# The x buffers at the top end of SBUF, a norm and sixteen weight copies on other engines, and the late weights' steps reordered

## Chip, cores and metric

The kernel runs on one core of one Trainium2 chip. The metric is the time of the whole program on the device in microseconds (us). Runs of the kernel before: median 1708.15 us of three (1706.96 to 1709.29).

## Reference

Block-diagonal attention (chunks of 64 tokens) makes x; two feed-forward stages follow, the first with relu squared, the second with a rational function as its activation.

```python
q_c = q.reshape(B, H, nc, chunk, D)                    # 8, 8, 9, 64, 64; k_c, v_c alike
scores = scale * np.matmul(q_c, k_c.transpose(0, 1, 2, 4, 3))
attn = np.exp(scores - np.max(scores, axis=-1, keepdims=True))
attn = attn / (np.sum(attn, axis=-1, keepdims=True) + 1e-09)
out = np.matmul(attn, v_c)                             # -> x: 4608 tokens x 512

h = x @ w_in1                                          # 512 -> 2048
x = np.maximum(h, 0.0) ** 2 @ w_out1                   # 2048 -> 512

h = x @ w_in2; h2 = h * h; h3 = h2 * h
P = a[0] + a[1] * h + a[2] * h2 + a[3] * h3
Q = 1.0 + np.abs(b[0]) * np.abs(h) + np.abs(b[1]) * h2
out = (P / (Q + 1e-6)) @ w_out2
```

## The kernel before

**Tiling.** The 4608 tokens are 9 blocks of 512 (4 attention tiles of 128 each), the 2048 inner columns are 16 slices f of 128. A step s is one block b and one f; both feed-forward stages have 9 x 16 = 144 steps. Every float32 operand of these products is split into a high part of the type fp32r and a low part (the difference), and each product is three matmuls: low x high, high x low, high x high (`mm3`, L179). So `mm_h` (L185), h = x @ w_in for one step, is 4 x 3 = 12 matmuls into one PSUM bank, with a w slice stationary and x moving (512 columns). `mm_out1` (L191) and `mm_out2` (L197) add a step's contribution to four accumulators (acc), 12 matmuls as well: in stage 1 a w slice is stationary and g moves, in stage 2 a slice of g is stationary and w moves. TensorE runs h of step s and then acc of step s - 2 (stage 1) or s - 3 (stage 2), as `LAG` says. There are 2 x 2 x 144 such groups of 12.

**Order.** Nothing is left to a scheduler. `at(t, fn, ...)` puts an event at a time counted in steps, and `issue(until)` runs all events below that time in order of (time, place in the list); this order is the order of every engine's queue. An event's time says nothing of when its inputs are there: an engine works its queue in order and waits at each instruction for what it needs. All loads and stores go through SyncE's (SP) one queue.

**Weights.** The inputs w_in and w_out are 32 weight tiles of 512 columns, named (f, half): half 0 is a piece of w_in, half 1 a slice of w_out. h of a step reads two half 0 tiles (for f = 14 and 15 these are (14, 0) and (15, 0)); acc of a step reads the half 1 tile of its f. A weight comes as 64-bit words. `w_load` (L126) fetches them into a staging tile st (two buffers, once the early ones are through), `w_words` (L138) is two ScalarE (ACT) passes, `w_join` (L146) one VectorE (DVE) pass that joins the halves into wc, `w_split` (L151) copies the high part on the engine given and subtracts on GpSimd (POOL) for the low part. The join frees the staging tile. Of the 32 tiles, 24 are early; 8 are late: their SBUF space is taken over from the staging tiles of the early ones. In the order in which the kernel before works on them they are (10,1), (11,1), (14,0), (15,0), (12,1), (13,1), (14,1), (15,1), at the times `t_late + 0.65 * jl` with t_late = 10.4, jl = 0 to 7; the load is 1.3 earlier, the join 0.4 and the split 0.8 later (L543 to L551). Even ones copy on ACT, odd ones on POOL.

**Attention.** It is spread over stage 1: per tile, two transposes or loads of q and k, scores (`mm_s`), max, exp, sum (`s_sum`, L339, whose last instruction makes z), `s_norm` (L345), a transpose of e, the product with v, and `x_evac` (L378), which writes a tile of x. For tiles 4 to 7 the norm is on POOL and e is transposed by TensorE (`f_tr`, L360), then copied by `f_copy` (L370), half on ACT and half on DVE; the tiles' q and k come by `tr_second` (L298). From tile 8 on the norm is on DVE. Their q and k come by `load_qk` (L266) in units of 192 tokens; unit 1 is 8 calls of 4 DMAs, so 32 pieces, at the event times 10.3 to 10.86.

**Passage to stage 2.** While stage 1's last block runs, `w_in2` and `w_out2`, joined earlier and kept in DRAM, are loaded into the same 32 tiles (`w2_load`); `w2_split` (L172) then copies the high part, half 0 on ACT and half 1 on DVE, and subtracts on POOL. Stage 2's activation is `e1` to `e4` (L390 to L431).

**SBUF.** From the bottom, a partition holds 384 bytes of scratch and constants, x (4 tiles of 8192), g (6 of 2048), r (2048), 24 early weights (4096 each, from 47,488 to 145,792), co (128 bytes), and from 145,920 the early staging tiles (32 KB), which the 8 late weights replace; in stage 2 t2 and ev lie where attention's pools at the right end were given up. The right end, where the pools with side="right" begin, is 229,344.

Of the kernel before, what the change touches and what calls it, by code (L numbers as in the profile page):

```python
# [26 lines left out]
def attn_moe_moe_kernel(  # L27
# [25 lines left out]
    nc = tc.nc  # L53
# [10 lines left out]
    NS = NBLK * NF  # L64
    scale = 1.0 / float(D) ** 0.5

    xs = ctx.enter_context(tc.tile_pool(name="xs", bufs=1))
    g_p = ctx.enter_context(tc.tile_pool(name="g", bufs=3))
    r_p = ctx.enter_context(tc.tile_pool(name="r", bufs=1))
    dram_p = ctx.enter_context(tc.tile_pool(name="scr", bufs=1, space=DRAM))  # L70
# [5 lines left out]

    w_order = sorted([(f // 2 * 2, f, 0) for f in range(NF)] + [(f + LAG[0] + 0.5, f, 1) for f in range(NF)])
    n_first, n_late = 2, 8
    late = [(half, f) for _, f, half in w_order[-n_late:]]
    W = {(half, f): const.tile([128, 2, DM], F32R, name=f"w{half}_{f}")  # L80
         for half in range(2) for f in range(NF) if (half, f) not in late}
# [8 lines left out]
    def at(t, fn, *args):  # L90
        events.append((t, len(events), fn, args))

    def issue(until):
        events.sort(key=lambda e: e[:2])
        with tc.manual_schedule():
            while events and events[0][0] < until:
                _, _, fn, args = events.pop(0)
                fn(*args)

    def tl(pool, shape, dt, nm, tag=None):  # L100
        return P[pool].tile(shape, dt, name=nm, tag=tag or nm)
# [396 lines left out]
    def attention(t, t0):  # L498
        if t < 2 * TPB:
            at(t0 - 1.45, tr_second, t)  # L500
            at(t0 - 1.2, tr_copy, t, "q", nc.vector)
            at(t0 - 1.2, tr_copy, t, "k", nc.vector)
        else:
            at(t0 - 1.0, tr, t, "qs", "q")
            at(t0 - 0.9, tr, t, "ks", "k")
        at(t0 - 1.5, load_tok, t, v, "v", f"v{t % 2}")
        at(t0, mm_s, t, t)
        at(t0 + 0.2, s_max, t)
        at(t0 + 0.45, s_exp, t)
        at(t0 + 0.6, s_sum, t)  # L510
        if t < 2 * TPB:
            at(t0 + 0.8, s_norm, t, nc.gpsimd)
            at(t0 + 1.5, f_tr, t, "aps")
            at(t0 + 1.6, f_copy, t)
        else:
            at(t0 + 0.9, s_norm, t, nc.vector)
            at(t0 + 1.1, s_tr, t)
# [6 lines left out]
    for t in range(TPB, NTILE + 1):  # L524
        b, i = divmod(t, TPB)
        slot[t] = slot1(i) if b == 1 else 14.9 + 3.14 * i if b == 2 else NF * (b - 1) - 4.55 + 4 * i
        at(slot[t], a_ps, t)
        if t > TPB:
            at(slot[t], mm_pv, t - 1, t)
            at(slot[t] + 0.3, x_evac, t - 1, nc.vector)  # L530
        if t < NTILE:
            attention(t, slot[t])

    for u in range(len(UNITS)):
        t0 = slot[(sum(UNITS[u - 2]) - 1) // 128] - 0.8 if u >= 2 else slot[2 * TPB - 2 + u] - 1.3
# [5 lines left out]
    t_late = -0.6 + 0.5 * (NF * 2 - n_late - n_first)  # L541

    for j in range(n_first, 2 * NF):  # L543
        key = w_keys[j]
        jl = j - (2 * NF - n_late)
        t = -0.6 + 0.5 * (j - n_first) if jl < 0 else t_late + 0.65 * jl
        if j >= 6:
            at(t - (1.3 if jl >= 0 else 2.6), w_load, *key)
        at(t, w_words, key)
        at(t + 0.4, w_join, key)  # L550
        at(t + 0.8, w_split, key, (nc.scalar, nc.gpsimd)[j % 2])  # L551

    for s in range(NS):
        at(s, mm_h, s)
# [12 lines left out]
    for f in range(NF):  # L567
        for half_, t in ((0, NS - NF + f // 2 * 2 + 1.6), (1, NS - NF + f + LAG[0] + 0.95)):
            at(t, w2_load, f, half_)
            at(t + 2.1 + (f * 0.3, f * 0.6)[half_], w2_split, f, half_, (nc.scalar, nc.vector)[half_])  # L570

    at(NS - 100, init2)
    for b in range(NBLK):
# [18 lines left out]
    def pool(stack, name, bufs, **kind):  # L592
        P[name] = stack.enter_context(tc.tile_pool(name=name, bufs=bufs, **kind))

    with ExitStack() as p1:
        pool(p1, "attn", 1, side="right")
        pool(p1, "w", 2, side="right")
        pool(p1, "wc", 2, side="right")
        pool(p1, "ev", 2, side="right")
        P["ident"] = tl("attn", [128, 128], F32, "ident")  # L600
        with ExitStack() as p0:
            pool(p0, "ws", 6)
            pool(p0, "wcs", 4)
            with ExitStack() as p00:
                pool(p00, "aps", 1, space=PSUM)
                issue(-10)
            pool(ctx, "acc", 1, space=PSUM)
            ACC += [P["acc"].tile([128, 512], F32, name=f"acc{i}", tag=f"acc{i}") for i in range(4)]
            pool(p1, "aps", 1, space=PSUM)
            issue(t_late + 0.35)  # L610
        pool(ctx, "wlate", 1)
        W.update({k_: P["wlate"].tile([128, 2, DM], F32R, name="w%d_%d" % k_, tag="w%d_%d" % k_) for k_ in late})
        issue(T_P2)
# [33 lines left out]
```

## Time and profile before

| what | value |
|---|---|
| median of three runs | 1708.15 us |
| profiled execution, time of the whole program | 1708.93 us |
| its span on the core | 1707.2 us |
| mean granted TensorE clock | 0.988 of full speed |
| TensorE (PE) busy | 1662.9 us, 97%, 9312 instructions |
| VectorE (DVE) busy | 1118.3 us, 66% |
| ScalarE (ACT) busy | 918.3 us, 54% |
| GpSimd (POOL) busy | 361.4 us, 21% |

How to read it: the profile is one execution, and its span is the time between the first and the last instruction on the core; the rest of the program's time lies around it. PE is TensorE's matmuls, PEld its weight loads, SPq the queue of SyncE, which issues the DMAs. L181 is line 181 of the kernel printed above. A row of the timeline gives the start, the duration and, in brackets, the idle time of that engine just before with what ended it. Stage 2 begins with step 144, and weights are exchanged between about 880 and 980 us.

### The profile page before, as it was taken

Reading aid. Unit: us, or ns where it says so; the run is one execution under the profiler, and the core shown is the slowest. Engines: PE = TensorE matmul, PEld = TensorE weight load, DVE = VectorE, ACT = ScalarE, POOL = GpSimd, SP = SyncE. Lnnn points to the kernel's source line nnn. Section 1 sums busy time; section 2 is a strip of 40 time slices with the busy share of each in tenths; the row PEclk is TensorE's granted clock in tenths of the full one; section 3 lists DMA queues with packets and bytes.
Section 4 is the critical chain, followed back from the end, with each engine's and each line's share of the span. In section 5 each row is a group of like instructions: output and inputs, shape, how many; then the busy total and the mean of one; then the engine's idle time right before and its main releaser. Section 6 shows DMA issues by size and latency. Waiting matters only on the chain.

```text
span 1707.2 us, 24454 instructions
## 1 busy us (share of the span) xinstructions
PE 1662.9 (97%) x9312; PEld 1352.2 (79%) x9312; DVE 1118.3 (66%) x1820; ACT 918.3 (54%) x1482; POOL 361.4 (21%) x290
## 2 busy tenths in 40 slices
PE   6898999999999999999999999999999999999998
PEld 4686888888788888888887788888888888888886
DVE  5765765556655566652118987777777777777776
ACT  5654333333333233322327677777777777777775
POOL 2542000000000000000565423232323232323222
PEclk8998999999999999999999999999999999999999
DMA  9544334334234343210431010101010101000000
GB/s 240 173 106 124 83 75 122 79 99 109 61 94 103 79 123 68 68 35 1 136 99 62 1 50 1 50 1 50 1 50 0 50 0 42 9 25 26 0 26 25
DMA packets 213190, 108.58 MB, mean 64 GB/s; under 512 B 182224, under 2 KB 182224, under 8 KB 211920
## 3 DMA queue, kind: packets, MB, share of 16 engines
q1 hardware_dynamic: 213072, 107.01, 23.3%
q8 instruction: 73, 1.20, 0.3%
q14 instruction: 45, 0.37, 0.1%
HBM read 79.69 MB, written 27.26 MB: 63 GB/s over the span
## 4 chain that ended last, share of the span: by engine, by line
PE 88%; DVE 6%; ACT 2%; DMA 1%; issue 1%; SPq 1%; POOL 0%; POOLq 0%; DVEq 0%; ACTq 0%
PE acc L181 15%; PE h L183 14%; PE h L181 14%; PE h L182 14%; PE acc L183 14%; PE acc L182 14%; PE a L323 1%; PE a L314 1%; DVE t L415 1%; DVE t L395 1%; SPq L272 1%; DVE w L416 1%; DVE wc L148 1%; DVE g L421 0%; DMA st<-in_moe_w_in_dram 0%
## 5 line engine op out<-in xcount | busy, mean ns | idle before, releaser
L181 PE MATMUL h<-x,w 128*128 128x512 f32 x1152 | 454.7, 395 | 13.4 <-DVE w L410 6.7
L182 PE MATMUL h<-x,w 128*128 128x512 f32 x1152 | 451.9, 392 | 0.4 <-DVE x L110 0.4
L183 PE MATMUL h<-x,w 128*128 128x512 f32 x1152 | 452.2, 393 | 0.0
L227 ACT ACTIVATE r<-h 128x512 f32<-128x512 f32 x144 | 86.0, 597 | 406.3 <-PE h L183 399.6
L110 POOL TENSOR_TENSOR gl<-g,gh 128x512 fp32r<-128x512 f32 x144 | 186.4, 1295 | 548.1 <-ACT gh L105 540.0
L107 DVE CAST gh<-r 128x512 fp32r<-128x512 f32 x144 | 67.5, 469 | 314.8 <-ACT r L228 309.2
L181 PEld LDWEIGHTS h<-x,w 128*128 128x128 f32 x1152 | 217.9, 189 | 63.4 <-DVE w L410 9.3
L182 PEld LDWEIGHTS h<-x,w 128*128 128x128 f32 x1152 | 218.2, 189 | 47.6 <-DVE x L110 0.9
L183 PEld LDWEIGHTS h<-x,w 128*128 128x128 f32 x1152 | 217.9, 189 | 47.2
L181 PE MATMUL acc<-gh,w 128*128 128x512 f32 x576 | 231.1, 401 | 3.2 <-POOL w L110 2.0
L181 PE MATMUL acc<-w,gl 128*128 128x512 f32 x576 | 226.7, 394 | 1.6 <-POOL gl L110 1.6
L395 DVE SCALAR_TENSOR_TENSOR t<-h,co,t 128x512 f32<-128x512 f32 x144 | 125.2, 870 | 155.8 <-ACT t L394 155.7
L183 PE MATMUL acc<-gh,w 128*128 128x512 f32 x576 | 227.0, 394 | 0.0
L182 PE MATMUL acc<-gl,w 128*128 128x512 f32 x576 | 227.0, 394 | 0.0
L183 PE MATMUL acc<-w,gh 128*128 128x512 f32 x576 | 225.5, 391 | 0.0
L182 PE MATMUL acc<-w,gh 128*128 128x512 f32 x576 | 225.3, 391 | 0.0
L110 POOL TENSOR_TENSOR gl<-r,gh 128x512 fp32r<-128x512 f32 x16 | 21.6, 1350 | 693.0 <-DVE gh L107 693.0
L105 ACT ACTIVATE gh<-g 128x512 fp32r<-128x512 f32 x144 | 91.2, 633 | 96.7 <-DVE g L421 96.7
L181 PEld LDWEIGHTS acc<-gh,w 128*128 128x128 f32 x576 | 109.0, 189 | 29.4 <-POOL w L110 2.7
L181 PEld LDWEIGHTS acc<-w,gl 128*128 128x128 f32 x576 | 108.1, 188 | 29.0 <-POOL gl L110 2.4
L183 PEld LDWEIGHTS acc<-gh,w 128*128 128x128 f32 x576 | 109.1, 189 | 24.3
L182 PEld LDWEIGHTS acc<-gl,w 128*128 128x128 f32 x576 | 109.4, 190 | 22.6
(76 smaller groups left out, 2279.7 us busy)
## 6 DMA issues: line engine op xcount, KB each, us to landing
st<-in_moe_w_in_dram SPq DMA_DIRECT2D x32, 512.0 KB, 4.1
st<-in_moe_w_out_dram SPq DMA_DIRECT2D x32, 512.0 KB, 4.3
x2d<-ev SPq DMA_DIRECT2D x36, 256.0 KB, 2.4
x<-x2d SPq DMA_DIRECT2D x9, 1024.0 KB, 4.8
out_dram<-ev SPq DMA_DIRECT2D x36, 256.0 KB, 2.2
v<-in_v_dram SPq DMA_DIRECT2D x32, 256.0 KB, 4.3
w2d<-wc SPq DMA_DIRECT2D x32, 256.0 KB, 2.8
w<-w2d SPq DMA_DIRECT2D x32, 256.0 KB, 2.6
```

Source lines behind the costliest of these rows:

```text
L105: nc.scalar.activation(out=o, in_=x, func=ACTF.Copy)
L107: eng.tensor_copy(out=o, in_=x)
L110: eng.tensor_tensor(out=o, in0=x, in1=hi.bitcast(F32), op=ALU.subtract)
L148: nc.vector.scalar_tensor_tensor(out=c, in0=c, scalar=3, in1=st[:, :, 0], op0=ALU.logical_shift_left, op1=ALU.bitwise_or)
L181: nc.tensor.matmul(out=o, lhsT=al, rhs=bh, start=first and i == 0, stop=False)
L182: nc.tensor.matmul(out=o, lhsT=ah, rhs=bl, start=False, stop=False)
L183: nc.tensor.matmul(out=o, lhsT=ah, rhs=bh, start=False, stop=last and i == len(pairs) - 1)
L227: nc.scalar.activation(out=r, in_=ps, func=ACTF.Relu)
L272: nc.sync.dma_start(out=T[nm, "unit", u][32 * Q:32 * Q + 32, hp, :n // 32], in_=src[bb, 2 * hp + Q // 2, ss:ss + n, 32 * (Q % 2):32 * (Q % ...
L314: nc.tensor.matmul(out=o[half(c), h, p], lhsT=q_[half(h), p, half(c)], rhs=k_[half(h), p, half(c)], start=True, stop=True)
L323: nc.tensor.matmul(out=o[half(h), c, p], lhsT=v_[half(c), 2 * p + h], rhs=a_[h][half(c), :, p], start=True, stop=True)
L395: nc.vector.scalar_tensor_tensor(out=t, in0=h2, scalar=co[:, 5:6], in1=t, op0=ALU.mult, op1=ALU.add)
```

## The change

Five things are changed, none of which alters what is computed.

- The pool of x, xs, is put at the right end of SBUF. Everything on the left lies 32,768 bytes lower for that, and x starts at 196,576.
- The norm of tiles 4 to 7 is issued on DVE instead of POOL.
- The eight late weights are the same tiles, in the order (10,1), (14,0), (15,0), (11,1), (12,1), (13,1), (14,1), (15,1). Their steps are 0.6 apart instead of 0.65, the join 0.25 and the split 0.5 behind the words, and all eight copies of the high part are on ACT.
- The cut between the first part of the order, in which the early staging tiles live, and the second lies at 10.70 instead of 10.75.
- The 16 copies of half 1 in `w2_split` are on ACT instead of DVE.

```diff
-    xs = ctx.enter_context(tc.tile_pool(name="xs", bufs=1))
+    xs = ctx.enter_context(tc.tile_pool(name="xs", bufs=1, side="right"))
...
     n_first, n_late = 2, 8
+    w_order[-n_late + 1:] = sorted(w_order[-n_late + 1:], key=lambda u: (u[2], u[0]))
...
         if t < 2 * TPB:
-            at(t0 + 0.8, s_norm, t, nc.gpsimd)
+            at(t0 + 0.8, s_norm, t, nc.vector)
...
-        t = -0.6 + 0.5 * (j - n_first) if jl < 0 else t_late + 0.65 * jl
+        t = -0.6 + 0.5 * (j - n_first) if jl < 0 else t_late + 0.6 * jl
         if j >= 6:
             at(t - (1.3 if jl >= 0 else 2.6), w_load, *key)
         at(t, w_words, key)
-        at(t + 0.4, w_join, key)
-        at(t + 0.8, w_split, key, (nc.scalar, nc.gpsimd)[j % 2])
+        at(t + (0.4 if jl < 0 else 0.25), w_join, key)
+        at(t + (0.8 if jl < 0 else 0.5), w_split, key, nc.scalar if jl >= 0 else (nc.scalar, nc.gpsimd)[j % 2])
...
             at(t, w2_load, f, half_)
-            at(t + 2.1 + (f * 0.3, f * 0.6)[half_], w2_split, f, half_, (nc.scalar, nc.vector)[half_])
+            at(t + 2.1 + (f * 0.3, f * 0.6)[half_], w2_split, f, half_, nc.scalar)
...
-            issue(t_late + 0.35)
+            issue(t_late + 0.3)
```

## Rows read from the trace of the kernel before

**Rows 1.** The page, parts 1, 2 and 4: busy us, share of the span and instructions of each engine; the clock granted to TensorE in 40 slices of the span, in tenths of full speed; the chain of work that ended last, its shares by engine.

```profile
PE 1662.9 (97%) x9312; PEld 1352.2 (79%) x9312; DVE 1118.3 (66%) x1820; ACT 918.3 (54%) x1482; POOL 361.4 (21%) x290
PEclk8998999999999999999999999999999999999999
PE 88%; DVE 6%; ACT 2%; DMA 1%; issue 1%; SPq 1%; POOL 0%; POOLq 0%; DVEq 0%; ACTq 0%
```

**Rows 2.** What PE waits for, from the view of waits: the first three rows from the span's first 170 us, the last from 880 to 990 us. Columns: what waits, for what; us in total, times, the longest in us.

```profile
PE a L367 <- POOL e L347: 6.4, 2, 4.0
PE h L181 <- POOL w L110: 5.9, 1, 5.9
PE acc L181 <- POOL w L110: 2.0, 1, 2.0
...
PE h L181 <- DVE w L410: 6.7, 5, 2.5
```

**Rows 3.** One stretch of the passage to stage 2 in the view of windows: the stretch and its length; busy us and instructions of PE, PEld, DVE, ACT and POOL; the granted clock; the busy share of the DMA engines; GB/s.

```profile
940.00:960.00 20.00, 17.62 (x71) 14.34 (x72) 19.09 (x24) 13.94 (x23) 9.50 (x7) 0.91 0.00 1
```

**Rows 4.** The start of each group of 12 matmuls in a stretch of stage 2, from PE's timeline, by the group's first matmul: acc of f=9, h of f=13 (of the same block), acc of f=10, h of f=14, acc of f=11, h of f=15. The last row is the view of windows over the block of 16 steps to which they belong, with the columns of rows 3.

```profile
1058.09 0.39 PE L181 MATMUL acc<-w,gl 128*128 128x512 f32 x1
...
1060.81 0.39 PE L181 MATMUL h<-x,w 128*128 128x512 f32 x1
...
1063.53 0.40 PE L181 MATMUL acc<-w,gl 128*128 128x512 f32 x1
...
1066.32 0.40 PE L181 MATMUL h<-x,w 128*128 128x512 f32 x1
...
1069.11 0.40 PE L181 MATMUL acc<-w,gl 128*128 128x512 f32 x1
...
1071.91 0.40 PE L181 MATMUL h<-x,w 128*128 128x512 f32 x1
...
1011.85:1099.72 87.87, 87.87 (x386) 71.92 (x384) 67.79 (x99) 65.84 (x103) 25.75 (x20) 1.00 0.06 25
```

**Rows 5.** The timeline around the norm of tile 5, all engines. The last row is one line's instructions under L347, the norms on DVE of the tiles from 8 on: lowest, median and highest ns, first and last start.

```profile
77.35 0.20 DVE L343 RECIPROCAL z<-z 128x8 f32<-128x8 f32 x1
77.47 2.10 DVE L148 SCALAR_TENSOR_TENSOR wc<-wc,st 128x512 int32<-128x512 int32 x2
77.72 1.30 POOL L347 TENSOR_TENSOR e<-e,z 128x512 f32<-128x512 f32 x1 [2.22 <-DVE z L343]
...
78.16 0.63 ACT L105 ACTIVATE w<-wc 128x512 fp32r<-128x512 f32 x1 [2.12 <-DVE wc L148]
...
79.08 1.12 PE L367 MATMUL a<-ident,e 128*128 128x128 f32 x4 [3.96 <-POOL e L347]
...
84.38 0.63 PE L290 MATMUL a<-ident,qn 128*128 128x128 f32 x4 [0.61 <-DVE ah L107]
...
L347 DVE TENSOR_TENSOR e<-e,z x28: 684/692/694, 154.1 to 763.2; 128x512 f32<-128x512 f32 x28
```

**Rows 6.** SyncE's queue in the timeline, around the loads of (14,0) (at 112.11) and (15,0) (at 125.71).

```profile
112.11 0.39 SPq L131 DMA_DIRECT2D st<-in_moe_w_in_dram  x1
...
116.91 8.70 SPq L272 DMA_DIRECT2D ks<-in_k_dram  x16
125.71 0.39 SPq L131 DMA_DIRECT2D st<-in_moe_w_in_dram  x1
```

**Rows 7.** The timeline around the late weights, all engines: the join of (10,1); the first matmul of acc of f=11 in block 0; the first words' pass of (15,0); the high and the low part of (14,0); the first matmul of h of f=14; the twelfth of the same group; the first of h of f=15.

```profile
108.75 1.80 DVE L148 SCALAR_TENSOR_TENSOR wc<-wc,st 128x512 int32<-128x512 int32 x1
...
125.49 0.48 PE L181 MATMUL acc<-gh,w 128*128 128x512 f32 x1
...
129.73 0.66 ACT L141 ACTIVATE wc<-st 128x512 f32<-128x512 f32 x1 [10.24 <-DMA st<-in_moe_w_in_dram]
...
131.98 0.61 ACT L105 ACTIVATE w<-wc 128x512 fp32r<-128x512 f32 x1
...
132.67 1.71 POOL L110 TENSOR_TENSOR w<-wc,w 128x512 fp32r<-128x512 f32 x1 [10.12 <-ACT w L105]
...
134.44 0.80 PE L181 MATMUL h<-x,w 128*128 128x512 f32 x1 [5.90 <-POOL w L110]
...
139.31 0.63 PE L183 MATMUL h<-x,w 128*128 128x512 f32 x1
...
147.56 0.51 PE L181 MATMUL h<-x,w 128*128 128x512 f32 x1
```

**Rows 8.** The weights' high parts made by DVE in the passage to stage 2, as one line of the view of the tile w (lowest, median and highest ns, first and last start), and the timeline around one of them, ACT, DVE and POOL.

```profile
L107 DVE CAST w<-w x10: 420/1026/1074, 886.9 to 977.3; 128x512 fp32r<-128x512 f32 x10
...
926.75 0.58 ACT L393 ACTIVATE h<-h 128x512 f32<-128x512 f32 x1
926.92 1.30 POOL L110 TENSOR_TENSOR gl<-g,gh 128x512 fp32r<-128x512 f32 x1 [3.36 <-ACT gh L105]
927.23 0.68 ACT L394 ACTIVATE t<-h,co 128x512 f32<-128x512 f32 x1
...
927.47 1.03 DVE L107 CAST w<-w 128x512 fp32r<-128x512 f32 x1
...
928.42 0.74 DVE L395 SCALAR_TENSOR_TENSOR t<-h,co,t 128x512 f32<-128x512 f32 x1
929.09 1.78 DVE L415 SCALAR_TENSOR_TENSOR t<-t,r 128x512 f32<-128x512 f32 x1
```

## The prediction

> **What bounds the kernel now.** The page comes first: TensorE (PE) is busy 97% of the span and the chain of work that ended last is 88% PE, with the granted clock at full speed in nearly every slice [rows 1]. So only two things move the time: moments in which PE waits or runs at half clock, and the pace of its 6912 matmuls of 512 columns. The waits of PE show where it stands still: 6.4 us for the norm on POOL (two waits), 5.9 and 2.0 us for late weights, 6.7 us for VectorE (DVE) where stage 2 begins [rows 2]. After the longer of these waits the clock is low for a while: 0.91 of full speed on the mean in a stretch of the transition [rows 3].
>
> Then the pace. Each group is 12 matmuls on one PSUM bank, and the timeline gives group lengths by subtraction of starts [rows 4]: acc of f=9 2.72 us, h of f=13 2.72, acc of f=10 2.79, h of f=14 2.79, acc of f=11 2.80. PE is busy for the whole of such a block, at a clock of 1.00, so nothing waits [rows 4]. The slow groups are those that read one of the eight late weights, all others (not broken by attention work or an eviction) take 2.72. In h the late weight is the stationary operand, in stage 2's acc the moving one; both are slow. What differs is where these tiles lie. Height alone is unlikely: the weight of f=9 ends 128 bytes below that of f=10, one at 2.72 and one at 2.79, so its limit would have to lie in those 128 bytes. What co's 128 bytes do change is the offset against the other operand: x, g and the 24 early weights all start at 384 modulo 512, the late ones at 0.
>
> **The change, part by part.** I sum against the profiled execution, 1708.93 us (span 1707.2 and 1.73 around it); the median of the three runs shown is 1708.15, 0.78 less, and the forecast goes by that.
>
> *x at the top.* No instruction is added. Everything on the left moves down by 32,768 bytes, so g, early and late weights keep their offsets against each other; so do t2, ev and the pools that they replace, and no wait arises there. x itself starts at 196,576, that is 480 modulo 512: 96 bytes off the early weights, in each of the 16 h groups of a block. The trace shows two offsets only: 0 (2.72) and 128 either way (2.79 to 2.80). 96 is nearer to 128 than to 0, so I take the slow pace for h: 14 groups of f=0 to 13 that are fast today, 18 blocks, 0.075 us each = **+18.9 us** (0.07 to 0.08: 17.6 to 20.2). h of f=14 and 15 is already slow, acc stays as it is. Bounds: 0 if x's offset doesn't matter; below nothing, -18.9 by symmetry, since no row shows that 2.72 is the floor.
>
> *Norm of tiles 4 to 7 on DVE.* Tile 5 is the dear one [rows 5]. DVE ends z at 77.55; POOL's norm runs 77.72 to 79.02 and PE starts at 79.08. A norm on DVE takes 0.69 against 1.30, so the transposes start 0.8 us earlier. But two weight joins stand behind it on DVE and move by 0.69. The ScalarE (ACT) copy at 78.16 waits for the first join; two word steps, two activations and ACT's half of the ah copies follow it in ACT's queue, DVE's half comes later still, and PE's transposes at 84.38 wait for it. So 0.8 won at 79 is lost at 84. DVE no longer waits behind POOL's norm (the second join), but its next ops meet POOL's weight splits elsewhere. Tile 4 goes likewise with 0.2 won; tiles 6 and 7 are not waited for. I take **+0.3 us** (-0.8 to +1.2).
>
> *Late weights.* The order of SyncE's (SP) queue decides [rows 6]. Today: the load of (14, half 0) after the first 8 of 32 q/k pieces, the other 24, then at 125.71 the load of (15, half 0), whose words start on ACT at 129.73; behind those words ACT holds the copy of weight 14 (131.98) and POOL its low part (132.67 to 134.38), for which PE waits until 134.44 [rows 7]. New order by times of events: (10,1), (14,0), 4 q pieces, (15,0), 28 pieces, (11,1). Weights 14 and 15 are in time, but (11,1) now stands behind 28 pieces of 8.70 / 16 = 0.544 us, 15.2 us. (15,0) ahead of them needs the staging buffer that (10,1)'s join frees, today at 108.75 + 1.80 = 110.55, then up to 1.2 us later as the relu split of step 10 comes first. So (11,1) is issued at 126.2 to 127.5, words 4.0 us later; by today's starts ACT needs 131.98 - 129.73 = 2.25 for the words and the relu and square of step 12, then 0.6 for the copy, and POOL 1.7 [rows 7]: PE goes on at 134.7 to 136.1. It now stands before acc of f=11, ready at 125.49, one group earlier than today's wait. From there to h of f=15: three groups (8.2), attention (1.1) and 1.6 to 3.2 for half clock (today 11 spacings of matmuls right after the wait take 139.31 - 134.44 = 4.87, 0.443 each, where 2.72 / 12 = 0.227 is usual [rows 7]), so 145.6 to 148.4 against 147.56 today, where the second wait of 2.03 falls away. Mid: **-0.7 us** (-3.0 with the join as early as today and a short half clock, +1.5). The closer steps behind it gain nothing: what they start from has not landed. All eight casts on ACT instead of four lie in its idle time. The tile's last q/k loads come out within 2 us of today's and are not waited for by PE. Moving the cut from 10.75 to 10.70 moves no early weight's step across it.
>
> *The 16 half-1 casts on ACT.* Ten show as a group on DVE from 886.9 to 977.3, up to 1.07 us each [rows 8]. Follow one: POOL's gl holds until 928.22, so the cast (927.47) ends at 928.50 and the next op starts at 928.42. On ACT the extra copy (about 0.5 from start to start, as 926.75 to 927.23) goes ahead of the next step's activations, so t is ready at 927.23 + 0.68 + 0.5 = 928.41: the same moment. The POOL subtraction of that weight, now not waiting for DVE, follows gl at once and holds up the next DVE op instead of the one after (929.09, 1.78 against 0.69). So the cast was cover for a wait, not its cause. I take **-0.3 us** for the five waits (6.7 us); ends -3.5 (half of them gone [rows 2]) and +1.0 (subtractions that become ready earlier fall on steps that are now free).
>
> Sum: +18.9 + 0.3 - 0.7 - 0.3 = +18.2, so 1727.1 for an execution such as the profiled one and **1726 us** against the median.
>
> **Rivals.** *(a) x's place costs nothing*: the pace hangs on something else about late tiles. Against it: the same instruction has two paces by tile, with no wait [rows 4]. The Trainium skill, SBUF — State Buffer, section "SBUF: two separate sides", says that contention arises only at the port pair shared by VectorE and GpSimd and that PE has ports of its own and never waits; by that rule the x move is worth nothing. The rows give 2.72 and 2.79, so it doesn't tell the whole, yet it may hold for 96 bytes. Time: 0.3 - 0.7 - 0.3 = -0.7, 1707.5 (ends -7.3 and +3.7, most of it 1703.5 to 1711). *(b) Faster*: late tiles are slow for their place, x is not touched, and 32 KB lower they run at 2.72: 8 groups x 18 x 0.075 = -10.8, so 1696.7. It decides if late groups fall to 2.72. Against it the 128 bytes above; for it, that nothing shows x's sensitivity. *(c) Height after all, for x too*: +18.9 for h, -6 x 18 x 0.075 = -8.1 for acc: 1718.3. *(d) The late weights' steps do not come closer at all*, since SP's queue sets them; it is in my term already, worth 1.5 us either way.
>
> **How the numbers follow.** Forecast (own range 1719 to 1731): 0.43. (a) 0.35, of which 0.05 falls under 1704.7 and 0.03 over 1711.6; (b) 0.15; (c) 0.07. A measurement of this kernel tells about 0.2%, 3.4 us, from no change. Faster: 0.15 + 0.05 = 0.20. Same: 0.35 - 0.08 = 0.27. Slower: 0.43 + 0.07 + 0.03 = 0.53. The range 1703 to 1731 takes in the forecast, (a) and (c), and leaves out (b) and the tails.
>
> **What would show it.** x: h groups of f=0 to 13 at 2.79 to 2.80 in the timeline, a block of 16 steps near 89 us instead of 87.87 [rows 4]; at 2.72 the forecast is wrong by some 19 us and (a) stands; acc of f=10 to 15 at 2.72 means (b) or (c). Norm: the PE transposes near 79.08 come 0.8 earlier, those near 84.38 do not. Late weights: one PE wait of 9 to 10 us before acc of f=11, none before h of f=14. Casts: PE waits for L410 of 6 to 7 us in total again; if they fall under 4 us, DVE's own time was the cause and I was wrong there.

## The result and the profile after

The changed kernel takes 1731.06 us (median of 4 runs, 1730.01 to 1731.92) against 1707.56 for the kernel before (4 runs): 1.0132 times as long, 95% interval 1.0119 to 1.0145, +23.5 us. The forecast was 1726 with an own range of 1719 to 1731, inside a wider one of 1703 to 1731; the median stands 0.06 us above the upper end of both. The sign and the mechanism were right, but the main term, x at the top, was too small: +18.9 was forecast and the move of x alone measures +23.4.

In the changed kernel every line number is one higher than before (L182 is the first matmul of `mm3`). The page, the lines that answer to [rows 1]:

```profile
PE 1687.6 (98%) x9312; PEld 1354.6 (78%) x9312; DVE 1102.1 (64%) x1808; ACT 929.3 (54%) x1502; POOL 349.4 (20%) x282
...
PEclk8998999999999999999999999999999999999999
...
PE 91%; DVE 4%; ACT 2%; DMA 1%; issue 1%; SPq 1%; POOL 0%; POOLq 0%; DVEq 0%; ACTq 0%
```

PE is 24.7 us longer busy with the same 9312 matmuls at the same clock, and PE has a larger share of the chain that ended last. So the time is lost inside the matmuls, not between them. The span grew from 1707.2 to 1729.1. What PE waits for, whole run, answering to [rows 2]:

```profile
PE acc L182 <- POOL w L111: 8.8, 1, 8.8
PE a L368 <- DVE e L348: 5.1, 2, 3.0
PE h L182 <- DVE w L411: 5.0, 3, 2.6
```

Those waits have become shorter: 18.9 us in all, where the four rows of before come to 21.0. In the passage to stage 2 the clock is what it was [rows 3]:

```profile
940.00:960.00 20.00, 17.40 (x69) 13.71 (x68) 15.80 (x19) 14.57 (x24) 11.41 (x9) 0.91 0.00 0
```

The pace is what changed. PE's timeline in stage 2, the first matmul of the same groups as in [rows 4], that is acc of f=9, h of f=13, acc of f=10, h of f=14, acc of f=11, h of f=15, and after them the view of windows over one block of 16 steps, from its first h to that of the next block:

```profile
1069.28 0.40 PE L182 MATMUL acc<-w,gl 128*128 128x512 f32 x1
...
1072.04 0.40 PE L182 MATMUL h<-x,w 128*128 128x512 f32 x1
...
1074.86 0.39 PE L182 MATMUL acc<-w,gl 128*128 128x512 f32 x1
...
1077.66 0.40 PE L182 MATMUL h<-x,w 128*128 128x512 f32 x1
...
1080.45 0.40 PE L182 MATMUL acc<-w,gl 128*128 128x512 f32 x1
...
1083.25 0.40 PE L182 MATMUL h<-x,w 128*128 128x512 f32 x1
...
1088.85:1178.26 89.41, 89.41 (x386) 71.98 (x385) 67.33 (x99) 65.88 (x103) 25.70 (x20) 1.00 0.07 25
```

By subtraction, h of f=13 takes 2.82 us where it took 2.72; h of f=14, already slow, takes 2.79 as before. And acc of f=9 takes 2.76 where it took 2.72, although neither of its operands has moved against the other. The block takes 89.41 instead of 87.87, with PE busy throughout at a clock of 1.00.

From the starts of the first h of each block, before and after, the 21.9 us of the span lie as follows: +1.2 ahead of block 0, -0.5 in block 0, +8.4 in blocks 1 to 7, +1.5 in block 8, -0.9 in block 9 (the passage), +10.7 in blocks 10 to 16, +1.5 in the last. The first 1.2 are not the change's: that first h comes at 33.2 and at 34.2 in two of the kernels below that differ only in padding (shift_all and co_pad). Nor can block 0 be read to better than about 2 us from one trace. It takes 120.13 in the kernel before and 118.29 in casts_only, which differs only from stage 1's last block on; from acc of f=11 to h of f=15 the granted clock was 0.77 in the one and 0.83 in the other. (Lengths of blocks and of groups that stand in no row come from PE's matmuls in each trace, in order.)

The late weights. SyncE's queue, answering to [rows 6], and the timeline of ACT, POOL and PE, answering to [rows 7]:

```profile
113.08 0.38 SPq L132 DMA_DIRECT2D st<-in_moe_w_in_dram  x1
113.51 5.94 SPq L273 DMA_DIRECT2D qs<-in_q_dram  x12
119.50 8.21 SPq L273 DMA_DIRECT2D ks<-in_k_dram  x15
127.81 9.40 SPq L136 DMA_DIRECT2D st<-in_moe_w_out_dram  x4
```

```profile
131.64 0.66 ACT L142 ACTIVATE wc<-st 128x512 f32<-128x512 f32 x1 [9.86 <-DMA st<-in_moe_w_out_dram]
...
133.89 0.61 ACT L106 ACTIVATE w<-wc 128x512 fp32r<-128x512 f32 x1
...
134.58 1.72 POOL L111 TENSOR_TENSOR w<-wc,w 128x512 fp32r<-128x512 f32 x1 [11.44 <-ACT w L106]
...
136.35 0.80 PE L182 MATMUL acc<-gh,w 128*128 128x512 f32 x1 [8.80 <-POOL w L111]
```

The load of (15,0) is out at 113.08, 27 pieces of q and k stand behind it, and the load of (11,1) is issued at 127.81. Two waits of 5.9 and 2.0 us have become one of 8.80, one group earlier.

### The profile page after: what moved, and what is told of

The parts are those of the page before. It is cut to its first block, busy times and chain, and to the rows that moved or that the text cites. A ratio compares the mean times of both kernels' runs of the same rounds, so it can differ in the third digit from the quotient of the medians.

```text
span 1729.1 us, 24450 instructions
## 1 busy us (share of the span) xinstructions
PE 1687.6 (98%) x9312; PEld 1354.6 (78%) x9312; DVE 1102.1 (64%) x1808; ACT 929.3 (54%) x1502; POOL 349.4 (20%) x282
## 4 chain that ended last, share of the span: by engine, by line
PE 91%; DVE 4%; ACT 2%; DMA 1%; issue 1%; SPq 1%; POOL 0%; POOLq 0%; DVEq 0%; ACTq 0%
PE acc L182 15%; PE h L183 15%; PE h L184 15%; PE h L182 15%; PE acc L183 15%; PE acc L184 14%; PE a L324 1%; PE a L315 1%; DVE wc L149 1%; SPq L273 1%; DMA st<-in_moe_w_out_dram 1%; DVE t L396 0%; DVE gh L108 0%; DVE w L417 0%; DVE t L416 0%
## 5 line engine op out<-in xcount | busy, mean ns | idle before, releaser
L182 PE MATMUL h<-x,w 128*128 128x512 f32 x1152 | 458.8, 398 | 5.9 <-DVE w L411 5.0
L184 PE MATMUL h<-x,w 128*128 128x512 f32 x1152 | 459.0, 398 | 0.0
L183 PE MATMUL h<-x,w 128*128 128x512 f32 x1152 | 458.5, 398 | 0.4 <-DVE x L111 0.4
L182 PEld LDWEIGHTS h<-x,w 128*128 128x128 f32 x1152 | 218.2, 189 | 59.9 <-DVE w L411 6.6
L182 PE MATMUL acc<-gh,w 128*128 128x512 f32 x576 | 232.5, 404 | 9.1 <-POOL w L111 8.8
L182 PE MATMUL acc<-w,gl 128*128 128x512 f32 x576 | 227.8, 395 | 1.6 <-POOL gl L111 1.6
L182 PEld LDWEIGHTS acc<-gh,w 128*128 128x128 f32 x576 | 109.4, 190 | 36.6 <-POOL w L111 9.0
L394 ACT ACTIVATE h<-h 128x512 f32<-128x512 f32 x144 | 86.0, 597 | 87.7 <-PE h L184 87.6
L182 PEld LDWEIGHTS acc<-w,gl 128*128 128x128 f32 x576 | 108.2, 188 | 31.0 <-POOL gl L111 2.4
```

Source lines behind the costliest of these rows:

```text
L182: nc.tensor.matmul(out=o, lhsT=al, rhs=bh, start=first and i == 0, stop=False)
L183: nc.tensor.matmul(out=o, lhsT=ah, rhs=bl, start=False, stop=False)
L184: nc.tensor.matmul(out=o, lhsT=ah, rhs=bh, start=False, stop=last and i == len(pairs) - 1)
L394: nc.scalar.activation(out=h2, in_=ps, func=ACTF.Square)
```

## The experiments

Two theories stood against each other. **Offset**: a group is slow when its stationary and its moving operand start at places that do not fit each other; x now starts 96 bytes off the early weights. **Place**: tiles far up in SBUF, or far from the weights, are slow, or the late weights are slow for how they are made. Beside them stood the question what the other parts of the change are worth. Where an interval is given the ratio is against the kernel before on the same chip.

**x_only: the move of x alone.**

```diff
-    xs = ctx.enter_context(tc.tile_pool(name="xs", bufs=1))
+    xs = ctx.enter_context(tc.tile_pool(name="xs", bufs=1, side="right"))
```

> The kernel before with x alone moved to the top end (480 modulo 512, everything else on the left 32,768 bytes lower). Offset theory (a group is slow when its stationary and its moving operand start at different places modulo 512): h of f=0 to 13 at 2.81 us, acc of f=0 to 9 at 2.76, 1.4 to 1.5 us more in each of the 18 blocks, so +25 to +26 us, 1733 us: more than the whole change, whose other parts then won 2 to 3 us. Rival, the other parts cost part of the +23.5: x alone gives less than +20, 1727 or under.

Measured: 1732.16 us against 1708.74, ratio 1.0138 (1.0124 to 1.0152), +23.4. A block of stage 2, by the view of windows:

```profile
1089.99:1179.41 89.42, 89.42 (x386) 71.99 (x385) 67.33 (x99) 65.89 (x103) 25.71 (x20) 1.00 0.07 24
```

This one line of the diff is the whole loss. The paces are as expected (h 2.815, acc of early f 2.758), but the sum is 2 us below the expectation: blocks 0 and 9 take 119.70 and 96.42 where they took 120.13 and 96.32, and the other sixteen together 22.3 more. That block 9 is no longer is not because PE's waits there became shorter: those for L410 are 7.8 us against 6.7. What differs is the clock. Block 9 by the view of windows, before and with x moved (the clock is the third figure from the end):

```profile
893.31:989.63 96.32, 89.66 (x373) 71.48 (x372) 82.42 (x99) 64.86 (x105) 47.28 (x34) 0.96 0.11 37
904.16:1000.58 96.42, 88.59 (x373) 69.16 (x372) 82.42 (x99) 64.98 (x105) 47.20 (x34) 1.00 0.11 36
```

The granted clock was 1.00 there instead of 0.96. As an estimate, 0.04 of 96 us leaves room for up to 4 us, more than the longer waits (1.1) and a block's slower pace (1.4 to 1.5) cost together; why the clock did not fall in this execution is open. Block 0 differs between traces by more than the pace costs, as said above.

**rest_only: everything but the move of x.**

```diff
-    xs = ctx.enter_context(tc.tile_pool(name="xs", bufs=1, side="right"))
+    xs = ctx.enter_context(tc.tile_pool(name="xs", bufs=1))
```

(against the changed kernel)

> The changed kernel with x put back at the left end: the norm, the late weights' steps, the cut and the sixteen copies alone. Offset theory: h of f=0 to 13 back at 2.72, and the time is that of before less 1 to 4 us (the waits for VectorE at the passage to stage 2 fall from 6.7 to about 5, the norm's from 6.4 to about 5, the late weights' go from 5.9 + 2.0 to about 8.8): 1703.5 to 1706.5. Rival, the other parts cost time of their own: 1708 to 1712.

Measured: 1707.89 against 1708.74, ratio 0.9995 (0.9986 to 1.0004). The other parts together are worth nothing that can be measured. The time is over the 1703.5 to 1706.5 that were expected, and 0.85 under its kernel before where 1 to 4 were. The waits named stand where they stand in the changed kernel (9.8 for the late weight, 5.4 in three for L411), and h of f=13 is back at 2.72.

**x_aligned: x at the top end, 96 bytes lower.**

```diff
+    ctx.enter_context(tc.tile_pool(name="xpad", bufs=1, side="right")).tile([128, 24], F32, name="xpad")
     xs = ctx.enter_context(tc.tile_pool(name="xs", bufs=1, side="right"))
```

(against the changed kernel; x starts at 196,480, 384 modulo 512)

> The changed kernel with 96 bytes of padding above x, so that x lies at the top end still but starts at 384 modulo 512, as g and the early weights do. Offset theory: h of f=0 to 13 at 2.72 and acc of f=0 to 9 at 2.72, the time of the changed kernel without its move of x, 1703 to 1707. Rival, the height of x or its distance from the weights: nothing changes, h stays at 2.81 and the time at 1731.

Measured: 1707.8 against 1708.74, ratio 0.9994 (0.9985 to 1.0003). PE's timeline: acc of f=9, h of f=13, acc of f=10, h of f=14.

```profile
1057.87 0.39 PE L183 MATMUL acc<-w,gl 128*128 128x512 f32 x1
...
1060.59 0.39 PE L183 MATMUL h<-x,w 128*128 128x512 f32 x1
...
1063.31 0.40 PE L183 MATMUL acc<-w,gl 128*128 128x512 f32 x1
...
1066.10 0.40 PE L183 MATMUL h<-x,w 128*128 128x512 f32 x1
```

acc of f=9 and h of f=13 take 2.72 each, acc of f=10 (late) 2.79; the time is 0.8 over the range expected. So 96 bytes of padding take back 23 us, with x still at the top end: height and distance of x count for nothing, and place falls as far as x goes.

**co_pad: co 512 bytes long in the kernel before.**

```diff
-    co = const.tile([128, 32], F32, name="co")
+    co = const.tile([128, 128], F32, name="co")
```

> The kernel before with co made 512 bytes long instead of 128, so that the eight late weights start at 384 modulo 512 as well. Offset theory: acc of f=10 to 15 and h of f=14 and 15 fall from 2.79 to 2.72, 8 groups x 18 blocks x 0.075 = 10.8 us less, 1697 us. Rival, late weights are slow for where they lie (high) or for how they are made: they stay at 2.79 and the time at 1707.5.

Measured: 1699.11 against 1708.74, ratio 0.9943 (0.9928 to 0.9958), -9.6. PE's timeline: acc of f=9, h of f=13, acc of f=10, h of f=14, acc of f=11, h of f=15; last a block of stage 2 by the view of windows.

```profile
1052.80 0.39 PE L181 MATMUL acc<-w,gl 128*128 128x512 f32 x1
...
1055.52 0.39 PE L181 MATMUL h<-x,w 128*128 128x512 f32 x1
...
1058.24 0.39 PE L181 MATMUL acc<-w,gl 128*128 128x512 f32 x1
...
1060.96 0.39 PE L181 MATMUL h<-x,w 128*128 128x512 f32 x1
...
1063.68 0.39 PE L181 MATMUL acc<-w,gl 128*128 128x512 f32 x1
...
1066.40 0.39 PE L181 MATMUL h<-x,w 128*128 128x512 f32 x1
...
1071.84:1159.14 87.30, 87.30 (x385) 71.94 (x384) 67.79 (x100) 65.78 (x103) 25.70 (x20) 1.00 0.07 25
```

Late or early, every group not broken by other work takes 2.72. The late weights were slow for the 128 bytes of co ahead of them, not for how they are made or how high they lie (they now lie 384 bytes higher). The gain of 9.6 is 1.2 short of the 10.8 expected. From the first h on the profiled execution is 10.6 shorter, in all blocks but block 0 (120.13 in both), block 9 included (95.75 against 96.32); the first h itself came 1.1 later, which is not the edit's.

**shift_all: all tiles shifted together.**

```diff
+    ctx.enter_context(tc.tile_pool(name="xpad", bufs=1)).tile([128, 24], F32, name="xpad")
     xs = ctx.enter_context(tc.tile_pool(name="xs", bufs=1))
...
-    co = const.tile([128, 32], F32, name="co")
+    co = const.tile([128, 128], F32, name="co")
```

> The kernel before with co 512 bytes long and 96 bytes of padding below x, so that x, g, early and late weights all start at 480 modulo 512. Offset theory (what counts is the difference between the two operands of a matmul): every unbroken group at 2.72, as with co made longer alone, 1697 to 1701 us. Rival, an absolute place (384 modulo 512 is fast for a tile and other places are slow, by itself): every group is slow, 2.79 to 2.82, 32 groups x 18 blocks x 0.075 to 0.095 = 43 to 55 us over the fast one, 1740 to 1755.

Measured, one run: 1699.33 us. A block of stage 2:

```profile
1071.78:1159.12 87.34, 87.34 (x385) 71.92 (x384) 67.75 (x100) 65.79 (x103) 25.69 (x20) 1.00 0.07 24
```

At 480 modulo 512, the very place at which x was slow, every group not broken by other work is fast when everything is there. It is the difference between the two operands that counts.

**x_off256 and x_off32: x 256 and 32 bytes off the early weights.**

```diff
+    ctx.enter_context(tc.tile_pool(name="xpad", bufs=1, side="right")).tile([128, 88], F32, name="xpad")
     xs = ctx.enter_context(tc.tile_pool(name="xs", bufs=1, side="right"))
```

(against the changed kernel; x_off32 has 32 instead of 88)

> The changed kernel with 352 bytes of padding above x: x starts at 128 modulo 512, 256 bytes off the early weights. Two forms of the offset theory: if the pattern repeats every 256 bytes, h of f=0 to 13 at 2.72 and the time at 1708; if every 512, h slow at 2.79 to 2.82 and the time at 1728 to 1733. The weights of f=14 and 15, at 0, are 128 off x in either case and tell whether 128 the other way round is as slow: 2.79 to 2.80.

> The changed kernel with 128 bytes of padding above x: x starts at 352 modulo 512, 32 bytes off the early weights. If only an exact match is fast: h of f=0 to 13 at 2.79 to 2.82, 1728 to 1733 us. If the price grows with the offset (96 bytes cost 0.095 us a group): a third of it, 2.75, some 1716. If a misfit under 64 bytes costs nothing: 2.72, 1708.

Measured, one run each: 1708.79 and 1728.13. The timeline of x_off256 (h of f=13, acc of f=10, h of f=14, acc of f=11), then that of x_off32 (acc of f=9, h of f=13, acc of f=10), each with a block of stage 2 by the view of windows:

```profile
1060.59 0.39 PE L183 MATMUL h<-x,w 128*128 128x512 f32 x1
...
1063.31 0.40 PE L183 MATMUL acc<-w,gl 128*128 128x512 f32 x1
...
1066.10 0.40 PE L183 MATMUL h<-x,w 128*128 128x512 f32 x1
...
1068.89 0.40 PE L183 MATMUL acc<-w,gl 128*128 128x512 f32 x1
...
1077.29:1165.19 87.90, 87.90 (x385) 71.91 (x384) 67.75 (x99) 65.85 (x103) 25.73 (x20) 1.00 0.07 24
```

```profile
1068.67 0.39 PE L183 MATMUL acc<-w,gl 128*128 128x512 f32 x1
...
1071.41 0.40 PE L183 MATMUL h<-x,w 128*128 128x512 f32 x1
...
1074.22 0.39 PE L183 MATMUL acc<-w,gl 128*128 128x512 f32 x1
...
1088.19:1177.29 89.10, 89.10 (x385) 72.00 (x384) 67.42 (x99) 65.87 (x103) 25.73 (x20) 1.00 0.07 25
```

256 bytes off is as fast as no offset (h of f=13 2.72). So the operands need not agree modulo 512, by which the prediction reckoned: 256 bytes apart is a fit as well. 32 bytes off, h of f=13 takes 2.81 by the rows (2.802 as the median of seven blocks) and acc of f=9 2.74: the price does not grow in proportion to the offset, most of it is there at 32.

**norm_only: the norm of tiles 4 to 7 on DVE.**

```diff
-            at(t0 + 0.8, s_norm, t, nc.gpsimd)
+            at(t0 + 0.8, s_norm, t, nc.vector)
```

> The kernel before with the norm of tiles 4 to 7 on VectorE and nothing else. Theory of the prediction (what the norm gains at tile 5 is lost at the next transposes, behind the weight joins): the first wait of PE on e falls from 4.0 to about 3.2, a new wait of 1 to 3 us for the ah copy appears before the transposes that follow, block 0 within 0.5 us of 120.1. Rival, the gain is kept: block 0 shorter by 0.8 to 1.3, no new wait.

Measured: 1710.12 against 1709.82, ratio 1.0000 (0.9991 to 1.0008). The timeline at tile 5, answering to [rows 5]:

```profile
77.44 0.69 DVE L347 TENSOR_TENSOR e<-e,z 128x512 f32<-128x512 f32 x1
78.04 1.29 DVE L148 SCALAR_TENSOR_TENSOR wc<-wc,st 128x512 int32<-128x512 int32 x2
78.28 0.73 PE L367 MATMUL a<-ident,e 128*128 128x128 f32 x4 [3.29 <-DVE e L347]
...
78.77 0.63 ACT L105 ACTIVATE w<-wc 128x512 fp32r<-128x512 f32 x1 [2.88 <-DVE wc L148]
...
83.70 0.87 DVE L107 COPY ah<-a 64x256 f32<-64x256 f32 x2
...
84.83 0.63 PE L290 MATMUL a<-ident,qn 128*128 128x128 f32 x4 [1.58 <-DVE ah L107]
```

PE starts on e at 78.28 instead of 79.08, the 0.8 us that the prediction gave. The ACT copy behind the join moves from 78.16 to 78.77, and the next transposes start at 84.83 instead of 84.38, after a wait of 1.58 on ah instead of 0.61. The gain is given back six microseconds later, and a little more. That is steady from trace to trace where block 0 as a whole is not: from PE's transposes of q and k for tile 5 to those for tile 7 it is 47.31 to 47.35 us in six kernels with the norm on POOL (before, late_only, casts_only, co_casts, co_pad, shift_all) and 47.63 to 47.67 in five with it on DVE (norm_only, rest_only, x_aligned, x_off256, best_a), so 0.3 us more.

**late_only: the late weights' order, spacing and copies, and the cut.**

```diff
+    w_order[-n_late + 1:] = sorted(w_order[-n_late + 1:], key=lambda u: (u[2], u[0]))
...
-        t = -0.6 + 0.5 * (j - n_first) if jl < 0 else t_late + 0.65 * jl
+        t = -0.6 + 0.5 * (j - n_first) if jl < 0 else t_late + 0.6 * jl
...
-        at(t + 0.4, w_join, key)
-        at(t + 0.8, w_split, key, (nc.scalar, nc.gpsimd)[j % 2])
+        at(t + (0.4 if jl < 0 else 0.25), w_join, key)
+        at(t + (0.8 if jl < 0 else 0.5), w_split, key, nc.scalar if jl >= 0 else (nc.scalar, nc.gpsimd)[j % 2])
...
-            issue(t_late + 0.35)
+            issue(t_late + 0.3)
```

> The kernel before with the late weights' order, spacing and copies and the cut at 10.70, nothing else. Theory of the prediction (SyncE's queue decides, the load of (11, half 1) stands behind 28 q/k pieces): one wait of 8.5 to 10 us before acc of f=11, none before h of f=14 or acc of f=14, block 0 within 1 us of 120.1. Rival, the closer steps bring the weights sooner: waits of under 6 us in all and a block 0 of under 118.

Measured: 1709.54 against 1709.82, ratio 0.9999 (0.9990 to 1.0008). The timeline at the one wait:

```profile
130.34 0.66 ACT L142 ACTIVATE wc<-st 128x512 f32<-128x512 f32 x1 [10.15 <-DMA st<-in_moe_w_out_dram]
...
133.28 1.72 POOL L111 TENSOR_TENSOR w<-wc,w 128x512 fp32r<-128x512 f32 x1 [10.28 <-ACT w L106]
...
135.05 0.80 PE L182 MATMUL acc<-gh,w 128*128 128x512 f32 x1 [9.48 <-POOL w L111]
```

One wait of 9.48 before acc of f=11, none at h of f=14. Block 0 takes 119.58, 0.55 less than before, which is within what block 0 differs by without any edit (118.29 in casts_only).

**casts_only and co_casts: the sixteen copies of half 1 on ACT**, alone and with the longer co.

```diff
-            at(t + 2.1 + (f * 0.3, f * 0.6)[half_], w2_split, f, half_, (nc.scalar, nc.vector)[half_])
+            at(t + 2.1 + (f * 0.3, f * 0.6)[half_], w2_split, f, half_, nc.scalar)
```

> The kernel before with the sixteen half 1 copies on ScalarE and nothing else. Theory of the prediction (the copy on VectorE was cover for a wait of the next operation on GpSimd's subtraction): PE's waits for L410 at 6 to 7 us as before, the passage from the start of block 9 to that of block 10 at 96.0 to 96.4, the time within 0.5 us of the kernel before. Rival (VectorE's own time was part of the cause, as the runs with all parts but x let one suspect): waits near 5.4 in three instead of five, the passage at 95.1, 1.2 us less.

> The kernel before with co 512 bytes long and the sixteen half 1 copies on ScalarE, norm and late weights as before. If the copies are all that the other parts give: the longer co's time less 1.2 us, so the same as with all parts, 1696 to 1698. If norm and late weights' steps help as well: over 1698.

Measured: casts_only 1708.42 against 1709.82, ratio 0.9993 (0.9985 to 1.0002); co_casts 1698.72, ratio 0.9934 (0.9921 to 0.9947). PE's waits for L410 in casts_only, from its timeline:

```profile
911.54 0.50 PE L181 MATMUL h<-x,w 128*128 128x512 f32 x1 [0.26 <-DVE w L410]
...
919.62 0.79 PE L181 MATMUL h<-x,w 128*128 128x512 f32 x1 [2.31 <-DVE w L410]
...
940.70 0.80 PE L181 MATMUL h<-x,w 128*128 128x512 f32 x1 [2.98 <-DVE w L410]
```

Before there were five, 6.7 us in all; the two long ones (2.53 and 2.50) have stayed, two short ones have gone. The waits are thus the rival's of casts_only. Block 9 takes 95.83, under the 96.0 to 96.4 of the prediction's theory and over the rival's 95.1. Without the copies it is 96.32 to 96.70 in three kernels (before, norm_only, late_only), with them 95.10 to 95.83 in four (casts_only, rest_only, x_aligned, x_off256); with the longer co it is 95.75 and 95.87 without (co_pad, shift_all), 94.57 and 94.60 with them (best_a, co_casts). So the copies are worth about 0.5 to 1.6 us in block 9, which the times alone do not tell from nothing. By its time co_casts falls on the side of "over 1698", that norm and late weights help as well; its own runs go from 1694.66 to 1700.21, so that is not shown.

**best_a: the kernel with all parts but the move of x, and the longer co.** The edit is that of rest_only and that of co_pad.

> All parts of the change but the move of x, and co 512 bytes long: every unbroken group at 2.72. By the two runs before, 1707.9 - 9.6 = 1698 us; if the parts other than x are worth anything it is under 1699.1, the time of the longer co alone, but by no more than 2.

Measured: 1696.88 against 1709.34, ratio 0.9929 (0.9916 to 0.9943). It is 0.7% under the kernel before and 2.0% under the changed one (1731.06, from other runs). It is also 2.2 under co_pad's time where at most 2 were expected, but its interval and those of co_pad and co_casts overlap: what is shown to be won is won by the 384 bytes that make co longer.

## Why the prediction came out as it did

**x at the top: mechanism right, term too small.** This term is the step that failed. Predicted +18.9, measured +23.4 for x alone. It was mis-sized in three places. The step "96 is nearer to 128 than to 0, so I take the slow pace" gave 0.075 us a group; 96 bytes cost 0.095 (2.815 against 2.72). The step "acc stays as it is" failed: the spacings of an acc group that follows a slow h group run irregularly, 224 to 236 ns, for about eight matmuls before they settle at 227; a group loses 0.038 so, nine a block. And of "18 blocks" sixteen became longer in the trace of x_only; that blocks 0 and 9 did not goes, as far as the rows tell, with the clock in block 9 and the spread of block 0 and not with the change, and it kept the loss some 3 us smaller. For one block of stage 2, on the mean of blocks 10 to 16 of x_only against before: ten h groups (f=4 to 13) 0.95; h of f=0 to 3, which had taken 2.735 and not 2.72 before, 0.28; nine acc groups 0.34; the six late acc groups 0.04; less 0.08 for the first acc (2.90 to 2.82): 1.53, and measured 89.41 - 87.88 = 1.53, where the prediction's 14 x 0.075 gives 1.05.

**Its reason.** That x's offset against the weights decides is shown by x_aligned, co_pad and shift_all together. "Modulo 512" was too coarse: 256 apart fits as well. The lower bound of -18.9 was empty: no offset here is faster than 2.72. Why an offset costs time is not settled. The rows show that PE waits for no other engine in these groups, and the recorded weight loads take 188 ns in slow and in fast groups alike. Each load starts together with the matmul before its own; within a group the operands of both lie in the same tiles, so no run tells whether it is a matmul's own stationary operand or the next one's that has to fit.

**Rival (a), x's place costs nothing,** falls with x_only. The Trainium skill, SBUF — State Buffer, section "SBUF: two separate sides", holds that on the engines' side only the port pair shared by VectorE and GpSimd gives contention and that PE waits for no one. Of waits of PE for another engine's access these groups show none; but taken as a reason to call placement free it fails here, by 2.815 against 2.72 us a group. **Rivals (b) and (c)**, late tiles slow for their height, fall with the changed kernel itself: 32 KB lower, acc of f=10 and of f=11 still take 2.80. What the prediction said against them, the 128 bytes between two weights of different pace, was the deciding argument.

**Norm.** Predicted +0.3, measured +0.3 between the transposes of tiles 5 and 7: right, and by the chain named (join, ACT copy, ah, transposes).

**Late weights.** Predicted -0.7; block 0 of late_only is 0.55 shorter, but that close a match is luck. From acc of f=10 to the end of block 0 the seven kernels with the old steps take 31.86 to 34.17 us and the seven with the new ones 32.45 to 33.71, so no size is shown. The order of things is: the queue decides, as said: PE went on at 135.05 there (134.7 to 136.1 predicted), in the changed kernel at 136.35, where the first h of block 0 had come 1.34 later already (34.31 against 32.97). So rival (d) holds: the closer steps bring nothing closer. h of f=15 started at 146.87 in late_only (145.6 to 148.4 predicted; by the prediction's own terms, 136.1 + 8.2 + 1.1 + 3.2, the upper end is 148.6).

**Copies.** Predicted -0.3, measured about -0.5 to -1.6 in block 9. "PE waits for L410 of 6 to 7 us in total again" failed: they are 5.0 in the changed kernel and 5.6 in casts_only, though not under the 4 that was to prove DVE's own time the cause. "The cast was cover for a wait, not its cause" holds for the two long waits, which stayed; that VectorE's own time was the cause of the two short ones that went fits and is not shown apart.

**Sum of the three small parts:** -0.7 predicted; rest_only gives -0.85, with an interval that includes no change, so the agreement tells little.

## What to carry to other kernels

Before a pool is moved, compute where each tile that a matmul reads starts, and compare the stationary with the moving operand modulo 256 bytes; pad until they agree. A small constant (here 128 bytes) ahead of a large pool can cost more than a whole round of moved instructions gains. Look for it in the pace of equal groups on an engine that never waits: two group lengths with no wait and a full clock were here the sign of data placement. And follow a saving next to a stall to the next stall: the 0.8 us of the norm were lost there again.

## What the runs showed of the hardware

The pace of twelve matmuls of 128x128 by 128x512 in fp32r at the full clock depends on the difference between the starts of the stationary and of the moving operand in a partition. Of the differences tried only 0 and 256 bytes are fast, which are the same modulo 256; others than these were not tried. The lengths are medians of blocks 10 to 16, and what the rows give as 2.79 by subtraction is 2.797 so.

| moving less stationary, modulo 512 | modulo 256 | run and group | one group, us |
|---|---|---|---|
| 0 | 0 | kernel before, h of f=13; shift_all, all unbroken groups | 2.720 |
| 256 | 0 | x_off256, h of f=13 | 2.720 |
| 96 | 96 | changed kernel, h of f=13 | 2.815 |
| 352 | 96 | x_off32, h of f=14 | 2.798 |
| 128 | 128 | x_off256, h of f=14 | 2.797 |
| 384 | 128 | kernel before, h of f=14 | 2.797 |
| 480 | 224 | x_off32, h of f=13 | 2.802 |
| 480 | 224 | changed kernel, h of f=14 | 2.796 |

The differences among the slow groups are small, and 480 gives two of them, so the size of the price is not set by the difference alone. It holds with the weights stationary (h, and acc of stage 1) and with them moving (acc of stage 2): in the kernel before, acc of f=10 takes 2.796 in stage 1 and 2.791 in stage 2. A slow group also slows the fitting group after it: by 0.015 us (h of f=0 to 3 in the kernel before), 0.024 (acc of f=9 in x_off32) and 0.038 (acc of f=9 in the changed kernel).
